# Forty-two unread products behind the last sums of an mLSTM and expert kernel

## The chip, the cores and the metric

The kernel runs on one core of a Trainium2 chip. The metric is device microseconds of one execution, from launch to end. The kernel before took 611.28 us, the median of two runs (610.89 and 611.67). The profile shows one execution, with the hardware profiler's start and length of each instruction. PE is the matrix engine (TensorE), PEld its loads of the stationary operand, DVE, ACT and POOL are VectorE, ScalarE and GpSimd, and SP is the engine that issues the output's transfers.

## The reference

Three stages follow one another. The first is a gated recurrence over 768 steps for 2 x 8 heads of width 40; its 1536 x 320 result goes through four experts that are weighted by given probabilities, and then through a gated pair of products:

```
for e in range(E):                       # w1[e] 320x1024, w2[e] 1024x320
    h = np.maximum(x @ w1[e], 0.0)
    out += p[:, e:e + 1] * (h @ w2[e])
a = x @ w_a                              # 320x1536
b = x @ w_b
return (a * b @ w_out).astype(np.float32)
```

## The kernel before

The weights come in 14 blocks: blocks 0 to 7 hold the experts, blocks 8 to 13 the gated pair. Every float32 operand of a large product is held as a rounded high part and a low part in the type fp32r (`wh` and `wl` for weights, `xh` and `xl` for the input of a stage, `hh` and `hl` for the hidden values), and a product is made of three: high by high, high by low, low by high. The 1536 rows are worked in three groups `c` of 512.

From block 3 on a unit is one block with one group `c` (the list `units`, line 836). A unit first makes its hidden values with `quad_a` (line 228: 60 products with 64 partitions of contraction and 512 columns, issued in pairs on the upper and the lower half of the array), and then, with `quad_b` (line 253: 48 products of 320 columns, in pairs too), the output sums of the unit before it. `evict` (lines 827 to 833) turns sums into `hh` and `hl` on ACT and DVE. `done2` adds finished output sums to the array `acc` on DVE (line 811) and, after block 13, issues the transfer of 128 rows of `acc` to the output from SP's queue (line 815).

The last unit has no unit behind it, so its output sums are made by the loop of lines 868 to 876: four tiles of 128 rows, each of six products over the full 128 partitions and 320 columns (lines 873, 874 and 875), then `done2`. These 24 products are PE's last work. Sums lie in PSUM banks from the pools `pa` and `pb`; `pb` takes turns between two pools of two banks each, and the four of them hold the `py` tiles of the last `quad_b` (line 855). Before the first instruction of the recurrence the manual order is switched on for the rest of the kernel (`ctx.enter_context(tc.manual_schedule())`), so each engine runs its instructions in the order of the program text. Products that are never read exist already: those of `warm_up` (line 626, 17 products of zeros in bf16 with 512 columns over the full array, all with one stationary operand and into one bank). Line 975 is the end of the program: each engine drains, SP waits for the counters of the transfers, and POOL collects the engines and lets them go.

Further lines that the prediction uses: line 208, products of blocks 0 to 2 over the full array with 256 columns; line 527, products of the recurrence with 82 columns whose moving operand starts 41 floats later from head to head; and line 583, the update of the recurrence's state:

```
for g in range(3):
    nc.tensor.matmul(pu[0:120, g * 123:(g + 1) * 123], kw[:, 3 * g:3 * g + 3, :].rearrange("p h d -> p (h d)"), kv[:, NK + g * 123:NK + (g + 1) * 123], ...)
```

There the stationary operand steps by 480 bytes and the moving operand by 492 bytes from one group to the next.

Of the kernel before, what the change touches and what calls it, by code (L numbers as in the profile page):

```python
# [7 lines left out]
F32 = mybir.dt.float32  # L8
# [10 lines left out]
P = 128  # L19
# [29 lines left out]
def mlstm_moe_kernel(ctx, tc, gates, qk, qc, kvo, dp, w1b, w2b, ident_d, bdmask_d, rsel_d, exp_d, out):  # L49
    nc = tc.nc  # L50
# [14 lines left out]
    xh = [xp.tile([P, 3, 512], F32R, name=f"xh{c}") for c in range(3)]  # L65
# [227 lines left out]
    def add_expert(blk, n, ps):  # L293
        e = blk // 2
        if blk <= 1:
            nc.scalar.activation(acc[n], ps, AF.Copy, scale=pg[:, n, 0:1])
        else:
            nc.vector.scalar_tensor_tensor(acc[n], ps, pg[:, n, e:e + 1], acc[n], op0=ALU.mult, op1=ALU.add)
# [491 lines left out]
    pa, pb = Turns(ps_a2, ps_a), Turns(ps_b2, ps_b)  # L790
# [11 lines left out]
    def done2(blk, n, ps):  # L802
        if blk < NB1:
            add_expert(blk, n, ps)
            if blk == NB1 - 1:
                twice[n] = hp2.tile([P, P], F32, tag="twice", name="twice", bufs=4)
                nc.scalar.copy(twice[n].rearrange("p (a b) -> p a b", a=2), acc[n][:, 256:].unsqueeze(1).to_broadcast([P, 2, 64]))
        elif blk == NB1:
            nc.scalar.copy(acc[n], ps)
        else:  # L810
            nc.vector.tensor_tensor(acc[n], ps, acc[n], op=ALU.add)
            if blk == NB1 + NB2 - 1:
                j, b = n // 2, n % 2
                r0 = b * S + j * P
                nc.sync.dma_start(out[r0:r0 + P, :], acc[n])
# [22 lines left out]
    for u, (blk, c) in enumerate(units):  # L838
# [9 lines left out]
        ps = [pa.tile([P, 512], F32, tag="a", name="psa" if blk < NB1 or g % 2 else "psb") for g in range(4)]  # L848
# [18 lines left out]
    wh, wl = wblk[blk]  # L867
    for t in range(4):
        ps = pa.tile([P, 512], F32, tag="a", name="psy")[:, 0:DM]
        for f in range(2):  # L870
            hh, hl = (x[:, t * P:(t + 1) * P] for x in h[f])
            off = f * WF2 + 768
            nc.tensor.matmul(ps, hh, wh[:, off:off + DM], start=f == 0, stop=False)
            nc.tensor.matmul(ps, hh, wl[:, off:off + DM], start=False, stop=False)
            nc.tensor.matmul(ps, hl, wh[:, off:off + DM], start=False, stop=f == 1)
        done2(blk, 4 * c + t, ps)


# ---- launch: one core; the host lays the inputs out
# [99 lines left out]
```

## Time and profile before

| | us |
|---|---|
| timed runs | 610.89 and 611.67, median 611.28 |
| span of the profiled execution, first to last instruction | 609.31 |
| PE busy in that span | 598.1 (98%) |
| DVE, ACT, POOL busy | 406.5, 277.9, 193.3 |
| PE's last product ends | 605.86 |
| from there to the end of the span | 3.45 |

The profiled execution has no time of its own beside its span; the median of the timed runs lies 1.97 us above the span. Starts are given in us from the start of the span. In a timeline each row has the start, the length, the engine, the line and operation with what it writes and reads, the shapes and the count of instructions merged into it. Products overlap in PE's pipeline, so the time that a product takes from its successor is the distance between two starts, not its length.

### The profile page before, as it was taken

The page shows a single profiled execution, that of the slowest core. Times are in us where ns is not written, and L with a number is a line of the kernel's source. Part 1 is how long each engine was busy: PE and PEld are TensorE (multiplying, and loading weights), DVE is VectorE, ACT ScalarE, POOL GpSimd, SP SyncE. Part 2 cuts the span into 40 slices and gives each one's busy share as a digit, 9 for nine tenths or more (in the row PEclk, how much of TensorE's full clock was granted, in tenths as well). Part 3 has the DMA queues.
Part 4 walks back from the last instruction along what each step waited for, and adds up shares of the span by engine and source line. Part 5 has one row for each costly group of instructions (what it writes and reads, how often), then busy time and mean ns, then how long its engine had stood idle before and what let it go on. Part 6 is the DMA issues. An engine that isn't in the chain of part 4 may idle for free.

```text
span 609.3 us, 14397 instructions
## 1 busy us (share of the span) xinstructions
PE 598.1 (98%) x5815; PEld 564.5 (93%) x5815; DVE 406.5 (67%) x829; ACT 277.9 (46%) x643; POOL 193.3 (32%) x233
## 2 busy tenths in 40 slices
PE   8799999999999999999999999999999999999997
PEld 5699999999999899999999999988898988888886
DVE  6898868676553333333789899898776787864344
ACT  7687476756533323333344344454553434331211
POOL 5486426363501011334233333333222222310000
PEclk9999999999999999999999999999999999999999
DMA  8877463737202122222222222222111120200002
GB/s 247 214 219 202 128 181 103 197 104 200 58 19 64 39 62 80 72 75 79 56 76 69 63 75 56 59 63 65 47 50 45 38 56 20 60 16 1 2 31 100
DMA packets 29351, 51.63 MB, mean 85 GB/s; under 512 B 3485, under 2 KB 18117, under 8 KB 29285
## 3 DMA queue, kind: packets, MB, share of 16 engines
q1 hardware_dynamic: 15925, 26.32, 15.9%
q10 hardware_dynamic: 12448, 22.03, 13.2%
q0 software_dynamic: 912, 2.36, 1.4%
q8 instruction: 45, 0.74, 0.5%
q14 instruction: 21, 0.17, 0.1%
HBM read 47.92 MB, written 2.00 MB: 82 GB/s over the span
## 4 chain that ended last, share of the span: by engine, by line
PE 92%; DVE 3%; POOL 1%; issue 1%; DMA 1%; ACT 1%; SPq 0%; DVEq 0%; POOLq 0%
PE psy L253 27%; PE psa L228 27%; PE psb L228 11%; PE psa L208 10%; PE psy L287 3%; PE psy L289 3%; PE psy L288 3%; PE pt_y L527 3%; PE pt_c L513 1%; PE pt_i L533 1%; POOL wl L93 1%; PE pt_u L583 1%; DMA acc<-in_w1b 1%; PE pt_x L145 0%; DMA gt<-in_gates 0%
## 5 line engine op out<-in xcount | busy, mean ns | idle before, releaser
L228 PE MATMUL psa<-xh,wh 64*128 64x512 f32 x576 | 135.2, 390 | 0.0
L253 PE MATMUL psy<-wl,hh 64*128 64x320 f32 x752 | 131.3, 305 | 0.0
L253 PE MATMUL psy<-wh,hh 64*128 64x320 f32 x752 | 131.3, 305 | 0.0
L253 PE MATMUL psy<-wh,hl 64*128 64x320 f32 x752 | 131.2, 305 | 0.0
L228 PE MATMUL psa<-xh,wl 64*128 64x512 f32 x414 | 97.4, 389 | 0.0
L253 PEld LDWEIGHTS psy<-wh,hh 64*128 64x128 f32 x752 | 85.7, 184 | 0.8
L228 PEld LDWEIGHTS psa<-xh,wh 64*128 64x128 f32 x576 | 80.9, 184 | 5.9 <-issue 0.9
L253 PEld LDWEIGHTS psy<-wl,hh 64*128 64x128 f32 x752 | 85.5, 184 | 0.8
L253 PEld LDWEIGHTS psy<-wh,hl 64*128 64x128 f32 x752 | 85.7, 184 | 0.0
L228 PE MATMUL psa<-xl,wh 64*128 64x512 f32 x384 | 85.6, 389 | 0.0
L828 DVE SCALAR_TENSOR_TENSOR hl<-psa,hh 128x512 fp32r<-128x512 f32 x60 | 38.6, 685 | 55.2 <-ACT hh L827 54.9
L125 POOL TENSOR_TENSOR wl<-tp,lf 128x272 fp32r<-128x272 f32 x48 | 38.8, 809 | 113.1 <-DVE tp L124 111.4
L228 PE MATMUL psb<-xh,wh 64*128 64x512 f32 x216 | 69.8, 389 | 0.0
L228 PEld LDWEIGHTS psa<-xh,wl 64*128 64x128 f32 x414 | 60.7, 184 | 3.7
L228 PE MATMUL psb<-xh,wl 64*128 64x512 f32 x180 | 58.5, 389 | 0.0
L228 PEld LDWEIGHTS psa<-xl,wh 64*128 64x128 f32 x384 | 55.2, 184 | 3.6
L122 POOL TENSOR_TENSOR lf<-lf,sq 128x272 f32<-128x272 f32 x48 | 38.1, 794 | 62.9 <-ACT wh L121 48.9
L276 DVE SCALAR_TENSOR_TENSOR hl<-psa,hh 128x256 fp32r<-128x256 f32 x72 | 30.3, 421 | 40.4 <-ACT hh L275 40.0
L93 POOL TENSOR_TENSOR wl<-raw,wh 128x352 fp32r<-128x352 f32 x28 | 26.4, 947 | 95.1 <-ACT wh L91 68.6
L275 ACT ACTIVATE hh<-psa 128x256 fp32r<-128x256 f32 x72 | 27.6, 383 | 59.2 <-PE psa L208 58.5
L827 ACT ACTIVATE hh<-psa 128x512 fp32r<-128x512 f32 x60 | 32.6, 596 | 44.7 <-PE psy L253 26.6
L208 PE MATMUL psa<-xh,wh 128*128 128x256 f32 x216 | 51.5, 293 | 0.3 <-ACT xh L133 0.3
(146 smaller groups left out, 1435.1 us busy)
## 6 DMA issues: line engine op xcount, KB each, us to landing
raw<-in_w2b ACTq DMA_DIRECT2D x48, 272.0 KB, 2.8
qk_t<-in_qk SPq DMA_DIRECT2D x16, 480.0 KB, 4.7
raw<-in_w1b ACTq DMA_DIRECT2D x32, 176.0 KB, 2.3
acc<-in_w1b SPq DMA_DIRECT2D x24, 176.0 KB, 4.0
kvo_t<-in_kvo SPq DMA_DIRECT2D x10, 364.5 KB, 7.1
Rr<-dL_t ACTq DMA_DIRECT2D x5, 512.0 KB, 6.3
og_t<-in_kvo SPq DMA_DIRECT2D x6, 320.0 KB, 4.6
out<-acc SPq DMA_DIRECT2D x12, 160.0 KB, 1.9
```

The source lines that it names most:

```text
L93: lo_eng.tensor_tensor(wl[:, cs], raw, wh[:, cs].bitcast(F32), op=ALU.subtract)
L122: nc.gpsimd.tensor_tensor(lf, lf, sq, op=ALU.mult)
L125: nc.gpsimd.tensor_tensor(wl[:, cs], tf, lf, op=ALU.add)
L208: nc.tensor.matmul(ps, l, r, start=(i == 0), stop=(i == len(prs) - 1))
L228: return nc.tensor.matmul(ps[g], w[rows, o:o + P], x, start=start, stop=stop)
L253: ms = [nc.tensor.matmul(ps[t], l[rows, t * P:(t + 1) * P], w[rows, off:off + DM], start=start, stop=stop) for t, rows in zip(two, (UP, DN))]
L275: nc.scalar.activation(self.hh, ps, AF.Relu)
L276: nc.vector.scalar_tensor_tensor(self.hl, ps, 0.0, self.hh.bitcast(F32), op0=ALU.max, op1=ALU.subtract)
L287: nc.tensor.matmul(ps, lh, wh[:, off:off + DM], start=(fi == 0), stop=False)
L288: nc.tensor.matmul(ps, lh, wl[:, off:off + DM], start=False, stop=False)
L827: nc.scalar.activation(hh, ps[f], AF.Relu)
L828: nc.vector.scalar_tensor_tensor(hl, ps[f], 0.0, hh.bitcast(F32), op0=ALU.max, op1=ALU.subtract)
```

## The change

Behind the loop the next turn of `pb` gives a bank to a new tile `ps_z`, and 42 products over the full array with 512 columns in fp32r are issued into it, each with start and stop set. `line` is `xh[2]` of the last group seen as 1536 columns in a row, `wh` is the high part of block 13's weights. The first 27 keep the moving operand at its start and move the stationary operand by 0, 8, ..., 64 floats (32 bytes a step), three products at each place; the other 15 keep the stationary operand and move the moving operand by 0, 8, ..., 32 floats. Nothing reads `ps_z`.

```
@@ -874,6 +874,11 @@
             nc.tensor.matmul(ps, hh, wl[:, off:off + DM], start=False, stop=False)
             nc.tensor.matmul(ps, hl, wh[:, off:off + DM], start=False, stop=f == 1)
         done2(blk, 4 * c + t, ps)
+    ps = pb.tile([P, 512], F32, tag="b", name="ps_z")
+    line = xh[2].rearrange("p a b -> p (a b)")
+    for w, x in [(8 * r, 0) for r in range(9)] + [(0, 8 * r) for r in range(5)]:
+        for _ in range(3):
+            nc.tensor.matmul(ps, wh[:, w:w + P], line[:, x:x + 512], start=True, stop=True)
```

## Rows read from the trace of the kernel before

**Rows 1.** The page: span and busy time of each engine with its share and instructions.
```profile
span 609.3 us, 14397 instructions
PE 598.1 (98%) x5815; PEld 564.5 (93%) x5815; DVE 406.5 (67%) x829; ACT 277.9 (46%) x643; POOL 193.3 (32%) x233
```

**Rows 2.** The page's 40 slices: busy tenths of PE, and its granted clock.
```profile
PE   8799999999999999999999999999999999999997
PEclk9999999999999999999999999999999999999999
```

**Rows 3.** Chain that ended last: start, us, what; its last pieces.
```profile
598.62 3.52 PE psy L253 x48
...
605.56 0.15 PE psy L874
605.71 0.16 PE psy L875
605.87 0.02 issue
605.89 0.49 DVE acc L811
```

**Rows 4.** The stretch behind PE's last product: length, then busy time by engine.
```profile
605.86:609.31 3.45, 0.00 (x0) 0.00 (x0) 0.49 (x1) 0.00 (x0) 0.00 (x0) 1.00 0.38 135
```

**Rows 5.** Timeline of the last sums: last of line 253, first and last of lines 873 to 875.
```profile
601.84 0.30 PE L253 MATMUL psy<-wh,hl 64*128 64x320 f32 x2
602.07 0.42 PE L873 MATMUL psy<-wh,hh 128*128 128x320 f32 x1
...
602.62 0.30 PE L873 MATMUL psy<-wh,hh 128*128 128x320 f32 x1
...
605.55 0.31 PE L875 MATMUL psy<-wh,hl 128*128 128x320 f32 x1
605.89 0.49 DVE L811 TENSOR_TENSOR acc<-psy,acc 128x320 f32<-128x320 f32 x1 [0.39 <-PE psy L875]
```

**Rows 6.** The page: the output's transfers, KB each, us from issue to landing.
```profile
out<-acc SPq DMA_DIRECT2D x12, 160.0 KB, 1.9
```

**Rows 7.** Line 975, the program's end: ns min/median/max, first and last start.
```profile
L975 SPq EVENT_SEMAPHORE  x12: 17/28/28, 606.8 to 609.2; - x12
L975 POOLq EVENT_SEMAPHORE  x4: 17/17/17, 608.6 to 609.2; - x4
...
L975 SPq DRAIN  x3: 7/7/13, 608.5 to 608.8; - x3
...
L975 PEldq DRAIN  x2: 13/1420/2828, 603.1 to 608.8; - x2
```

**Rows 8.** Line 626, unread products: ns min/median/max, first and last start, forms.
```profile
L626 PEld LDWEIGHTS <-acc x17: 98/138/151, 1.4 to 20.1; 128*128 128x128 bf16 x17
L626 PE MATMUL pt_w<-acc x17: 379/609/634, 1.4 to 20.2; 128*128 128x512 bf16 x17
```

**Rows 9.** Chain, a typical unit: 30 pairs of 512 columns from line 228.
```profile
336.72 6.83 PE psa L228 x60
```

**Rows 10.** Timeline: line 228 in the last unit, 13 steps of a pair apart.
```profile
595.25 0.39 PE L228 MATMUL psa<-xh,wh 64*128 64x512 f32 x1
...
598.23 0.39 PE L228 MATMUL psa<-xh,wh 64*128 64x512 f32 x1
```

**Rows 11.** Timeline: five products of line 626 in a row, at full clock.
```profile
17.43 1.24 PE L626 MATMUL pt_w<-acc 128*128 128x512 bf16 x5
```

**Rows 12.** Timeline: line 208, full array, 256 columns, then the next line.
```profile
61.83 0.28 PE L208 MATMUL psa<-xh,wh 128*128 128x256 f32 x1
...
61.95 0.28 PE L208 MATMUL psa<-xh,wl 128*128 128x256 f32 x1
...
62.07 0.31 PE L287 MATMUL psy<-wh,hh 128*128 128x320 f32 x1
```

**Rows 13.** Line 875, loads of the stationary operand: columns as in the rows of line 626.
```profile
L875 PEld LDWEIGHTS psy<-wh,hl x8: 187/188/188, 602.3 to 605.4; 128*128 128x128 f32 x8
```

**Rows 14.** Line 583, operands at steps of 480 and 492 bytes: loads and products.
```profile
L583 PEld LDWEIGHTS pt_u<-kvo_t,kw_t x60: 181/183/186, 32.3 to 144.3; 128*120 128x120 f32 x60
L583 PE MATMUL pt_u<-kvo_t,kw_t x60: 266/268/271, 32.4 to 144.4; 128*120 128x123 f32 x60
```

**Rows 15.** Timeline: one run of line 583, six products merged.
```profile
51.71 0.80 PE L583 MATMUL pt_u<-kvo_t,kw_t 128*120 128x123 f32 x6
```

**Rows 16.** SP's waits from 606 us on: us in total, times, longest.
```profile
SPq L975 <- DMA out<-acc: 1.1, 3, 0.5
```

## The prediction

> **What bounds the kernel now.** I read the page first. PE is busy for 598.1 of 609.3 us [rows 1], and its slices are full from end to end at full granted clock, the faster of its two levels, 2.4 GHz [rows 2]. So work that is added to PE lengthens the kernel unless it falls into a stretch where PE has nothing to do. The chain of waits says where such a stretch lies: it is a string of PE's products up to the last one of line 875, then one addition on DVE [rows 3]. Behind that product, from 605.86 us to the end at 609.31, PE has no work at all [rows 4]. What fills these 3.45 us is the addition, which ends at 605.89 + 0.49 = 606.38 [rows 5], the last transfer of 160 KB, 1.9 us from issue to landing [rows 6], and the closing of the program [rows 7].
>
> The closing decides how much of that stretch is free for PE. PE's drain starts at 603.1 us, well ahead of the products, and lasts 2.83 us, to 605.9: it ends with the last product [rows 7]. SP then runs through its waits for counters from 606.8 us and drains at 608.5, and POOL begins to collect the engines at 608.6 [rows 7]; I read the moment from which everything hangs as 608.55. From there 0.76 us are left to the end of the span. PE may therefore finish 608.55 - 605.90 = 2.65 us later than now before it is the last that POOL waits for. That is the slack which the change can use up.
>
> **The change, part by part.** It removes and moves nothing, and every instruction that it adds is on PE: 42 loads of a stationary operand and 42 products. No transfer is added, and no queue is passed by another.
>
> *Do they run at all, and where?* Each engine follows the program text, so they stand behind the 24 products of lines 873 to 875. That an unread product is not left out is shown by line 626: all 17 of its products and all 17 of its loads are in the trace, though nothing reads their bank and all have one and the same stationary operand [rows 8]. So I count 42 loads too, not 14.
>
> *The first one.* Its bank belonged to the first `py` tile, which DVE has added up well before 605.7 us, and its operands were ready long ago; nothing is late for it. Where PE passes from line 253 to line 873, the step is 602.07 - 601.84 = 0.23 us instead of the usual 0.147 [rows 5]; I take these 0.08 us once, for the pass to a new bank with its waits. Behind the products only PE's drain is queued.
>
> *The step of one product.* The trace has no full-array fp32r product with 512 columns in a row of its own kind, so I bound it. Above: line 228 issues two halves of the array together with 512 columns each, 6.83 us for 30 pairs or 0.228 each [rows 9], and in the last unit 598.23 - 595.25 = 2.98 us for 13 steps, 0.229 [rows 10]. Below: five unread bf16 products of 512 columns over the full array into one bank take 1.24 us at full clock; without the last one's own length, 0.38, that is 0.86 / 4 = 0.215 [rows 11]. Between: 256 columns over the full array step by 0.12 [rows 12], 320 by (605.55 - 602.62) / 20 = 0.1465 [rows 5]; the line through both gives 0.1465 + 192 x 0.0265 / 64 = 0.226 at 512. I take 0.2287, the pairs', since 64 rows or 128 make no difference at 320 columns either: 48 products of line 253 in pairs take 3.52 us, 0.1467 a pair [rows 3]. The stationary loads last 188 ns [rows 13] and start beside the product before, so they stay hidden. Writing one bank again and again costs nothing in line 626.
>
> The Trainium skill, TensorE: Matmul & The Clock Gate, section Back-to-back issue gap, gives two figures for a warm product of 512 columns: 215.7 ns alone, and about 131 ns in a stream of loads and products. The first agrees with the lower bound from line 626; no row here shows 512 columns as short as the second. By 131 ns the 42 would take 5.5 us, of which 2.9 would show, and the time would be 614.1.
>
> *The addresses.* They are the open question. 24 products have a moved stationary operand and 12 a moved one on the other side; only 6 start both at the tiles' beginnings. The nearest rows are line 583, whose stationary operand steps by 480 bytes (a multiple of 32, not of 64) and whose moving operand steps by 492. Its loads last 181 to 186 ns and its products 266 to 271 over all three places [rows 14]: no place stands out, so the low end is nothing. The high end: a run's six products (each of its three calls leaves two in the trace) take 0.80 us [rows 15], without the last one's length (0.80 - 0.27) / 5 = 0.106 each for 123 columns, or 0.862 ns a column. If all of that were the reading of the moving operand, 512 columns would take 0.441 us, 0.212 more than 0.2287. For the 12 with a moved moving operand that is 2.5 us at most; if the stationary operand's address counted alike, 7.6 us for 36. I take nothing, as the lengths at the three places say.
>
> *The sum.* Added to PE: 42 x 0.2287 + 0.08 = 9.69 us. Less the slack of 2.65: 7.04 us. Step by step: the first would start at 605.55 + 0.147 + 0.08 = 605.78, the last 41 steps later at 615.16, and end 0.39 later at 615.55; PE's drain 0.04 behind it, then 0.76 for the closing: a span of 616.35 against 609.31. The difference goes on the median of the timed runs, which stands 1.97 us above the span for what lies around it: 611.28 + 7.04 = 618.3 us. If SP also waits for PE's new counter before its other entries, those come behind it: SP spends 608.5 - 606.8 = 1.7 us on its list, 1.1 of it waiting for transfers [rows 7, 16] that would be over by then, so up to 0.6 more. With the step of 0.215 the sum is 9.03 + 0.08 - 2.65 = 6.5.
>
> **The rivals.**
>
> *Shorter than the sum, or no change.* If the number of columns did not set the step, 42 products could go at 0.106 as in line 583: 4.45 + 0.08 - 2.65 = 1.9 us, 613.2. Against it: the steps grow with the columns, 0.12, 0.1465, 0.228 [rows 5, 9, 12]. The Trainium skill's 131 ns, named above, would lie between. To vanish wholly the products would have to be dropped, which line 626 speaks against, or step by 2.57 / 42 = 0.061, half of the shortest step seen; then 611.3. Together 3 in 100.
>
> *The moving operand's address costs a part.* The 12 products with a moved moving operand take up to 0.441 each: up to 618.3 + 2.5 = 620.9. For it speaks only that no row has an fp32r operand at 32 bytes from a 64-byte step; line 583 with its even lengths speaks against it. 9 in 100.
>
> *Slower by over 2%.* Any start away from the tile's beginning, of either operand, makes a product read its operand at half rate. Then 36 products take a second 0.2287: 8.2 us on top, 626.5. It decides from 12.2 us (2% of 611.28) on, that is from (12.2 - 7.04) / 36 = 0.144 more per product, 0.37 us a product. Line 583 allows up to 0.441 a product and so doesn't exclude it, but its loads of 181 to 186 ns at steps of 480 bytes show no trace of it. 6 in 100.
>
> **How the numbers follow.** The forecast, 42 products at 0.215 to 0.235 us and nothing for addresses, has 82 in 100 and gives 617.8 to 619.2; with the two runs' scatter of 0.4 us each way, and the upper bound of the moved moving operand, the range is 617.2 to 621.3. It leaves out the dropped or shortened products and the half rate, some 1 in 10, and a part of the second rival. Over or under 2%, 12.2 us, is about what a measurement of this kernel can tell from no change: the forecast is 1.2% longer, inside it. Slower by over 2% is the half rate alone, 0.06; for faster by over 2% I see no mechanism and leave 0.01; within 2% is the rest, 0.93.
>
> **What would show it right or wrong.** In the changed kernel's profile the 42 products should stand behind 605.7 us, with steps of 0.228 from first to last, the three at each place alike, at full granted clock. Loads should stay near 188 ns. PE should be busy some 608 us, its drain should end near 615.6, POOL's collecting start right behind it, and the chain of waits end on PE instead of on DVE's addition. DVE's last addition and the output's last transfer should stand where they are. Steps that widen where the moving operand moves, and stay there, would be the second rival; steps that widen at every moved place, the third. A stretch of idle time ahead of the first new product would mean a wait for the bank that I costed at 0.08 us.

## The result and the profile after

The changed kernel takes 618.24 us, the median of two runs (617.88 and 618.60), against 611.28: 1.011 times as long, 95% interval 1.0085 to 1.0135, or 5.2 to 8.3 us. The forecast was 618.3 with a range of 617.2 to 621.3, and within 2%.

The page of the changed kernel answers [rows 1]: the span is 7.6 us longer and PE's busy time 11.0 us, of which 9.7 lie in the new products; the rest lies ahead of them, where the two executions differ. The chain's end, in which [rows 3] had DVE's addition last, now has the 42 products last. Their 9.72 us are 0.2314 us a product.

```profile
span 616.9 us, 14480 instructions
...
PE 609.1 (99%) x5856; PEld 573.8 (93%) x5857; DVE 405.9 (66%) x829; ACT 277.6 (45%) x643; POOL 193.7 (31%) x233
```

```profile
605.89 0.15 PE psy L874
606.04 0.15 PE psy L875
606.19 9.72 PE ps_z L881 x42
```

The timeline shows the passage from the last sums to the new products, as [rows 5] showed the last sums: start, length, engine, line, operation, count. The first new product starts 0.14 us behind the last of line 875, with no gap, and DVE's last addition runs beside the new products. It stands 0.33 us later than before, as the last sums do: that much of the two profiled executions' difference arose ahead of the changed lines.

```profile
605.88 0.31 PE L875 MATMUL psy<-wh,hl 128*128 128x320 f32 x1
...
606.02 9.88 PE L881 MATMUL ps_z<-xh,wh 128*128 128x512 f32 x42
...
606.23 0.49 DVE L811 TENSOR_TENSOR acc<-psy,acc 128x320 f32<-128x320 f32 x1 [0.39 <-PE psy L875]
```

The new line's own rows (ns min/median/max, first and last start) answer [rows 13]: the loads take what they took in the last sums. The rows of the program's end answer [rows 7]; it is line 980 now. PE's drain starts at 611.6 and lasts 4.36 us, to 615.95, one of SP's waits lasts 6.58 us, and POOL begins to collect at 616.1. SP's waits answer [rows 16]: SP waits 6.6 us for the products that nobody reads.

```profile
L881 PEld LDWEIGHTS ps_z<-xh,wh x42: 187/188/189, 605.9 to 615.3; 128*128 128x128 f32 x42
L881 PE MATMUL ps_z<-xh,wh x42: 387/394/400, 606.0 to 615.5; 128*128 128x512 f32 x42
```

```profile
L980 SPq EVENT_SEMAPHORE  x12: 17/28/6582, 607.6 to 616.8; - x12
L980 POOLq EVENT_SEMAPHORE  x4: 17/17/17, 616.1 to 616.8; - x4
...
L980 PEldq DRAIN  x2: 13/2185/4357, 611.6 to 616.4; - x2
```

```profile
SPq L980 <- PE ps_z L881: 6.6, 1, 6.6
SPq L980 <- DMA out<-acc: 1.3, 3, 0.5
```

One thing changed that is not on PE. Of SP's twelve issues of the output's transfers (line 815), the longest took 0.435 us before and takes 1.453 us after; the first row is the kernel before, the second the changed one. Among the last eight transfers the median from issue to landing rose from 1.9 us, as in [rows 6], to 2.6.

```profile
L815 SPq DMA_DIRECT2D out<-acc x12: 332/372/435, 591.8 to 606.4; - x12
```

```profile
L815 SPq DMA_DIRECT2D out<-acc x12: 332/374/1453, 592.1 to 607.2; - x12
```

In the changed kernel's transfers between 602.9 and 604.6 us one packet of 16 KB on the queue of instructions stands beside the output's. The same stretch of the kernel before has none; its last packet on that queue starts at 610.59, behind the last instruction of the span.

```profile
q8 instruction: 1, 0.02, 4.7%
out<-acc SPq DMA_DIRECT2D x2, 160.0 KB, 3.2
```

### The profile page after: what moved, and what is told of

The parts are those of the page before. It is cut to its first block, busy times and chain, and to the rows that moved or that the text cites. A ratio compares the mean times of both kernels' runs of the same rounds, so it can differ in the third digit from the quotient of the medians.

```text
span 616.9 us, 14480 instructions
## 1 busy us (share of the span) xinstructions
PE 609.1 (99%) x5856; PEld 573.8 (93%) x5857; DVE 405.9 (66%) x829; ACT 277.6 (45%) x643; POOL 193.7 (31%) x233
## 4 chain that ended last, share of the span: by engine, by line
PE 93%; POOL 2%; issue 2%; DVE 2%; DMA 1%; SPq 0%; ACT 0%; POOLq 0%; DVEq 0%
PE psy L253 27%; PE psa L228 26%; PE psb L228 11%; PE psa L208 10%; PE psy L287 3%; PE psy L289 3%; PE psy L288 3%; PE pt_y L527 2%; PE pt_c L513 2%; POOL wl L93 2%; PE ps_z L881 2%; PE pt_i L533 1%; DMA qk_t<-in_qk 1%; PE pt_u L583 1%; POOL w_t L505 1%
## 5 line engine op out<-in xcount | busy, mean ns | idle before, releaser
L228 PE MATMUL psa<-xh,wh 64*128 64x512 f32 x576 | 133.5, 390 | 0.0
L253 PE MATMUL psy<-wh,hh 64*128 64x320 f32 x752 | 127.2, 305 | 0.0
L253 PE MATMUL psy<-wh,hl 64*128 64x320 f32 x752 | 127.1, 305 | 0.0
L253 PE MATMUL psy<-wl,hh 64*128 64x320 f32 x752 | 127.0, 305 | 0.0
L228 PEld LDWEIGHTS psa<-xh,wh 64*128 64x128 f32 x576 | 79.1, 184 | 5.9 <-issue 0.9
L253 PEld LDWEIGHTS psy<-wl,hh 64*128 64x128 f32 x752 | 81.5, 184 | 0.8
L253 PEld LDWEIGHTS psy<-wh,hh 64*128 64x128 f32 x752 | 81.4, 184 | 0.8
L253 PEld LDWEIGHTS psy<-wh,hl 64*128 64x128 f32 x752 | 81.6, 184 | 0.0
```

Of the source, the lines that this page charges most:

```text
L228: return nc.tensor.matmul(ps[g], w[rows, o:o + P], x, start=start, stop=stop)
L253: ms = [nc.tensor.matmul(ps[t], l[rows, t * P:(t + 1) * P], w[rows, off:off + DM], start=start, stop=stop) for t, rows in zip(two, (UP, DN))]
```

## The experiments

Theory A is the prediction's: columns set the step of a product, addresses cost nothing, and 2.65 us behind the last sums are free for PE. The rivals are a price of the addresses, a price that does not depend on columns or place, and, after the first results, a second effect that the new instructions have on SP. Experiments of one group ran on one chip beside the kernel before; the ratios are against those runs.

**All products at one place** (group one, with the next three).

```
-    for w, x in [(8 * r, 0) for r in range(9)] + [(0, 8 * r) for r in range(5)]:
-        for _ in range(3):
-            nc.tensor.matmul(ps, wh[:, w:w + P], line[:, x:x + 512], start=True, stop=True)
+    for _ in range(42):
+        nc.tensor.matmul(ps, wh[:, 0:P], line[:, 0:512], start=True, stop=True)
```

> All 42 products keep both operands at their tiles' beginnings; nothing else differs from the changed kernel. If addresses cost nothing, the 42 steps average 0.231 us as in the changed kernel and the time is the changed kernel's, 618.2 us, 1.011 times the kernel before. If a moved start costs a few nanoseconds, as the steps of 0.233 to 0.235 at some places hint against 0.228 at the beginning, all steps are 0.228 to 0.229, PE ends 0.1 us earlier, and the time is still 618.1.

Measured: 618.77 us, ratio 1.0108 (1.0089 to 1.0127), the changed kernel's. The chain gives 9.63 us for 42 products, 0.2293 each, against 0.2314:

```profile
607.16 9.63 PE ps_z L880 x42
```

So addresses decide nothing here, but they are not quite without a trace. The distances between starts, ns, repeat to the nanosecond: from the seventh product on this kernel goes 226, 229, 231 or 232 over and over, and the changed kernel and the kernel of the fourth experiment, with the same addresses, show one sequence from the third place to the last; some of it:

```
place (floats)            changed kernel     products ahead of the last sums
stationary from 16        226 227 235        226 227 235
stationary from 48        237 230 237        237 230 237
stationary from 64        226 229 232        226 229 232
moving from 24            232 234 238        232 234 238
```

A pattern that comes back in another kernel belongs to the places and not to chance. The kernel with 168 products below, on another chip, begins with the same twelve distances as this one. It is worth 231.27 - 229.15 = 2.1 ns a product on the mean of the steps, 0.09 us for the 42.

**Ten products instead of 42.**

```
-    for _ in range(42):
+    for _ in range(10):
```

The lines are those of the first experiment, all operands at their tiles' beginnings.

> Ten products instead of 42, both operands at their tiles' beginnings. 10 x 0.231 = 2.3 us is less than the 2.65 us by which PE's drain came before POOL's collecting. If that slack is free, the time is the kernel before's, 611.3 us (ratio 1.000). If products behind the last sums lengthen the closing whatever their number, it is 611.3 + 2.3 = 613.6 (ratio 1.004).

Measured: 612.71 us against 611.8, ratio 1.0013 (0.9998 to 1.0028). 1.004 is excluded, 1.000 is not. In the trace PE's drain ends at 608.51, 1.33 us ahead of POOL's collecting at 609.84, so the ten products are hidden, as theory A has it. But POOL's collecting stands 3.64 us behind the start of DVE's last addition, where it stood 2.66 in the kernel before, and one of SP's issues took 1.75 us. Something other than PE's work delayed the closing; the last three experiments are about that.

**256 columns instead of 512.**

```
-            nc.tensor.matmul(ps, wh[:, w:w + P], line[:, x:x + 512], start=True, stop=True)
+            nc.tensor.matmul(ps[:, 0:256], wh[:, w:w + P], line[:, x:x + 256], start=True, stop=True)
```

> The same 42 products at the same addresses with 256 columns instead of 512. If columns set the step, it is 0.118 to 0.120 us as on line 208, PE's new work is 5.0 us, and the time is 611.3 + 5.0 - 2.65 + 0.2 = 613.8. If a product has a fixed price by the instruction or by its stationary load, the step stays near 0.23 and the time near 618.2.

Measured: 613.46 us, ratio 1.0029 (1.0017 to 1.0040), or 1.0 to 2.4 us. The chain has 4.95 us for 42 products, 0.118 each, the step of line 208 in [rows 12]:

```profile
605.86 4.95 PE ps_z L881 x42
```

Its span of 611.79 is 2.48 us above the kernel before's, with the last sums at the same place to 0.01 us; the measured terms give 4.95 - 2.65 + 0.18 = 2.48 (the 0.18 is explained under the slack below). The 2.5 of the forecast is met in the trace and lies just above the interval of the times. Columns set the step, and a fixed price by instruction is refuted.

**The products ahead of the last sums.**

```
     wh, wl = wblk[blk]
+    ps = pb.tile([P, 512], F32, tag="b", name="ps_z")
+    ...
     for t in range(4):
```

> The same 42 products, put ahead of the loop of the last sums instead of behind it. If the 2.65 us behind the last sums is the only cover, nothing of 42 x 0.231 = 9.7 us is hidden here: 611.3 + 9.7 = 621.0, up to 0.4 more if the first product waits for DVE to add up the tile that held its bank. If the place does not matter, the time is 618.2.

Measured: 620.95 us, ratio 1.0151 (1.0134 to 1.0168), or 8.2 to 10.3 us. The span is 9.81 us above the kernel before's, so nothing is hidden here, as theory A says of this place. The timeline and the waits show the wait for the bank, too: 0.41 us from the last product of line 253 to the first new one, where it is 0.23 to line 873 in [rows 5], for DVE's addition that frees it. DVE's last addition is again the end of the chain.

```profile
601.77 0.30 PE L253 MATMUL psy<-wh,hl 64*128 64x320 f32 x2
602.18 0.74 PE L872 MATMUL ps_z<-xh,wh 128*128 128x512 f32 x2
```

```profile
PEld ps_z L872 <- DVE acc L811: 0.4, 1, 0.4
```

**The stationary operand's address with nothing to cover the load** (group two, this one and the next two, one run each).

```
+    for w in [8 * r for r in range(9)] + [1, 2, 3, 4, 5]:
+        for _ in range(6):
+            nc.tensor.matmul(ps[:, 0:64], wh[:, w:w + P], line[:, 0:64], start=True, stop=True)
```

> 84 products of 64 columns behind the last sums, all with the moving operand at its beginning, six at each of 14 starts of the stationary operand: 0, 8, ..., 64 floats, then 1, 2, 3, 4, 5 floats. With so few columns the step is the stationary load's own, about 0.107 to 0.112 us. If the load's address costs nothing, all 14 places step alike. If a load from an odd start takes longer and 512 columns only covered it, the places at 32 bytes from a multiple of 64, or those at 1 to 5 floats, step wider by more than 5 ns.

Measured: 622.16 us. The first six places, from 0 to 40 floats, step by 111 or 112 ns, but for the very first step. Then the granted clock falls from 1.00 to 0.50, and the other places, 48, 56, 64 and 1 to 5 floats, step by 213 to 215 ns once the clock is down, all alike again. The columns of the stretches are length, then busy time of PE, PEld, DVE, ACT and POOL, the granted clock, and the DMA's share and GB/s; the loads before and after the fall follow.

```profile
605.20:608.50 3.30, 3.30 (x32) 3.30 (x31) 0.49 (x1) 0.00 (x0) 0.00 (x0) 1.00 0.73 255
609.50:619.00 9.50, 9.50 (x46) 9.50 (x47) 0.00 (x0) 0.00 (x0) 0.00 (x0) 0.50 0.00 0
```

```profile
L881 PEld LDWEIGHTS ps_z<-xh,wh x30: 187/192/192, 605.0 to 608.3; 128*128 128x128 f32 x30
...
L881 PEld LDWEIGHTS ps_z<-xh,wh x47: 315/333/334, 609.2 to 619.0; 128*128 128x128 f32 x47
```

At neither clock can the places seen at it be told apart; starts of 1 to 5 floats were seen here at the lower clock alone. The half rate of the third rival is refuted for the stationary operand.

**Finer and more places.**

```
+    for w, x in [(0, x) for x in (0, 1, 2, 3, 4, 8, 16, 24, 32)] + [(w, 0) for w in (0, 1, 2, 3, 4)]:
+        for _ in range(12):
+            nc.tensor.matmul(ps, wh[:, w:w + P], line[:, x:x + 512], start=True, stop=True)
```

> 168 products of 512 columns behind the last sums, 12 at each place: moving operand from 0, 1, 2, 3, 4, 8, 16, 24, 32 floats, then stationary operand from 0, 1, 2, 3, 4 floats. If addresses cost nothing, each place averages 0.229 to 0.232 us, with the places in no order, and the time is 611.3 + 168 x 0.230 - 2.65 + 0.2 = 647.5. If a moved moving operand costs something, the places off the beginning stand together above the first by 3 ns or more.

Measured: 647.99 us where one run of the kernel before took 612.26, 35.7 us more; 36.2 were expected. The chain has 0.232 us a product:

```profile
606.29 38.97 PE ps_z L881 x168
```

The means of the steps at each place, ns, from the starts in the trace:

```
moving from      0: 230.0   1: 236.1   2: 235.1   3: 228.7   4: 230.7   8: 234.5   16: 232.8   24: 234.5   32: 233.1
stationary from  0: 229.8   1: 233.1   2: 230.3   3: 227.0   4: 232.4
```

The places off the beginning do not stand together above it: 3 floats are below 0, and 4 floats below 16 and 32. The largest difference is 9 ns, from 227.0 to 236.1. What sets these few nanoseconds stays open. In this one trace the distance from a multiple of 32 or 64 bytes does not order them: 3 floats, off both, step shorter than 16 and 32 floats, on both.

**The same words read as bf16.**

```
+    wb, xb = wh.bitcast(BF16), line.bitcast(BF16)
+    for _ in range(42):
+        nc.tensor.matmul(ps, wb[:, 0:P], xb[:, 0:512], start=True, stop=True)
```

> 42 products of 512 columns behind the last sums with the same words read as bf16. If the 0.215 us of line 626 belongs to the type, the step is 0.215 and PE's new work 9.1 us: 617.5. If it belonged to line 626's zeros or place, the step is 0.229 to 0.231 and the time 618.2.

Measured: 616.82 us where one run of the kernel before took 612.26. The steps are 215 or 216 ns, but for a first one of 442, where the trace lacks one product's record; the chain has the other 40 behind it. The time is 0.7 us under the expected one, and only 4.6 us above that one run, where 6.2 were expected; single runs cannot settle that. In this execution the last sums ended 0.8 us earlier than in the profiled one of the kernel before.

```profile
605.33 8.80 PE ps_z L881 x40
```

So the 0.215 us of line 626 belong to the type and not to its zeros or its place: with the same starts, columns and count fp32r steps by 0.229 and bf16 by 0.216. Read as bf16, 512 columns are only the first 256 of the words, half the bytes; whether the type or the bytes make the 13 ns is not separated.

**The fetch of instructions without products at the end** (group three, with the next two). Theory B: the new instructions make PE's stream cross into another 16 KB block just at the end, the block is fetched while the last transfers are issued, and that fetch holds up SP. Its rival: the products behind the last sums hold up SP. That the packets are PE's code is read from a count: the kernel with 168 products has 252 instructions more on PE than the changed kernel and one packet more on that queue (47 against 46), 16384 bytes or 65 for each. This kernel is the kernel before with five small unread products at the start and nothing at the end.

```
+        def small(n):
+            for _ in range(n):
+                nc.tensor.matmul(pw[:, 0:64], wz[:, 0:P], wz[:, 0:64], start=True, stop=True)
-            ... (-17.366, warm_up, 4), (-16.214, go, w0[2:3]),
+            ... (-17.366, warm_up, 4), (-17.3, small, 5), (-16.214, go, w0[2:3]),
```

> The kernel before, with nothing behind the last sums, and five more unread bf16 products of 64 columns at 17 us, where PE is idle for 1.2 us. They add ten instructions to PE's stream, so the 16 KB block of PE's instructions that before was fetched at 610.6 us, behind the end, should be fetched some 8 us earlier, near 602.6. If that fetch holds up SP's issue of an output transfer, one of the last eight issues takes 1.4 to 2.2 us instead of 0.33 to 0.40, POOL's collecting stands some 3.6 us behind the start of DVE's last addition instead of 2.66, and the time is 0.7 to 1.0 us longer (ratio 1.0014). If the slow issue in the runs so far comes from the products behind the last sums, all issues are short, the distance is 2.66 and the ratio 1.000.

Measured: the packet of instructions now starts at 602.98, and one of SP's issues (line 820 here) takes 1.128 us, with no product behind the last sums. The distance from DVE's last addition to POOL's collecting is 3.03 us instead of 2.66, less than the 3.6 expected. In the time it cannot be told: 611.47 against 611.33, ratio 1.0002 (0.9991 to 1.0014).

```profile
L820 SPq DMA_DIRECT2D out<-acc x12: 333/374/1128, 592.0 to 606.7; - x12
```

**Ten products, with the fetch moved away.** Ten products as in the second experiment, ten of the small ones at 17 us and twelve at 15.

```
+            ... (-29.623, s2a, 1, 0), (-29.5, small, 12),
+            ... (-17.366, warm_up, 4), (-17.3, small, 10), (-16.214, go, w0[2:3]),
```

> Ten products behind the last sums as in the earlier run of ten, and 22 more unread bf16 products of 64 columns at 15 and 17 us. The 44 instructions should move the fetch of PE's block to about 600 us, ahead of the last eight output transfers. If the fetch is what holds up SP, their issues take 0.33 to 0.40 us and POOL's collecting stands 2.7 us behind the start of DVE's last addition, with the ten products still behind the last sums; up to 1 us of new work may show in the first 20 us. If the ten products hold up SP, one issue takes 1.4 us or more and the distance is 3.6 us.

Measured: 610.89 us, ratio 0.9994 (0.9982 to 1.0006). The fetch lasts from 603.04 to 604.23, and the first of the last eight issues from 603.79 to 604.13, within it, at its usual 0.333 us; the second starts as the fetch ends. This profiled execution reached the last sums 1.6 us later than the kernel before. The longest issue takes 0.403 us, the median landing of the last eight is 1.8 us, and POOL's collecting stands 2.64 us behind the start of DVE's last addition, with ten products behind the last sums.

```profile
L820 SPq DMA_DIRECT2D out<-acc x12: 332/372/403, 593.4 to 608.0; - x12
```

**Ten products once more.**

> The ten products once more, beside the two kernels above. If the fetch theory holds, this one keeps its slow issue and 3.6 us from DVE's last addition to POOL's collecting, and lies 0.7 to 1.0 us above the kernel before (ratio 1.001 to 1.002). If the distance of the first look was chance, it is 2.7 us and the ratio 1.000.

Measured: 612.25 us, ratio 1.0014 (1.0000 to 1.0028). The fetch starts at 603.874 and SP's slow issue at 603.868; it takes 1.609 us, and the distance is 3.47 us.

```profile
L815 SPq DMA_DIRECT2D out<-acc x12: 333/374/1609, 592.6 to 607.8; - x12
```

The three kernels separate the two theories. A fetch in the middle of the issues gives a slow issue with ten products (1.75 and 1.61 us) and with none (1.13); ten products with the fetch over by the second issue give none.

The end of the fetch ties the two together more closely. From the starts and lengths in the traces, us:

```
                                 fetch             slow issue        ends behind the fetch by
fetch without products           602.98 to 604.14  603.26 to 604.39  0.25
changed kernel                   603.37 to 604.64  603.45 to 604.90  0.27
ten products once more           603.87 to 605.18  603.87 to 605.48  0.30
168 products                     603.58 to 605.40  603.56 to 605.78  0.38
```

In all ten kernels with a slow issue it ends 0.15 to 0.39 us behind the fetch, while the fetches last 1.15 to 1.82 us. It is not a matter of the program's end either: the kernel before has a case at 100 us, where the packet of instructions takes from 100.24 to 101.19 and the issue, of line 370, ends at 101.55.

```profile
100.46 1.09 SPq L370 DMA_DIRECT2D kvo_t<-in_kvo  x1
```

Through the twelve traces, 41 issues of SP follow another within 0.15 us and start between 0.12 us ahead of such a fetch and its end; 40 of them end 0.15 to 0.39 us behind it. Of some 800 that follow another as closely elsewhere, nine take over 0.7 us, and no fetch on this queue explains those. An issue after a longer pause can be short in the middle of a fetch, as the first of the last eight is in the second of these kernels.

That a fetch at this place holds up SP is shown, by moving it and by when the slow issue ends; by what means it does so is not. The price in the trace is 0.8 us between the closings of the second and the third of these kernels (3.47 less 2.64). The times agree: of the second kernel's twelve, ten lie below all twelve of the third (medians 610.89 and 612.25).

## Why the prediction was right, point by point

**The work on PE.** 42 x 0.2287 + 0.08 = 9.69 us was forecast. Measured are 42 x 0.2313 = 9.71, with 0.2313 the mean distance between the starts from 606.025 to 615.507. Two small errors cancelled, which is luck: the step was 2.6 ns longer, and the 0.08 us for the pass to the new bank were not there. The 0.23 us step from line 253 to line 873, from which they were taken, is still there in the changed kernel (602.17 to 602.40), so it belongs to that passage and not to a new bank as such: the load of line 873 starts only with its product there, while the first new load starts at 605.88, beside the last product of line 875.

**The step's bounds.** The value from the pairs of line 228, between their 0.2277 and 0.2292 [rows 9, 10], was right to 1%, the line through 256 and 320 columns, 0.226, to 2.3%, and the bf16 rows [rows 11] were a lower bound for the reason that the type, and with it the bytes, differs. The figure of 131 ns for 512 columns in a stream that the Trainium skill gives (TensorE: Matmul & The Clock Gate, Back-to-back issue gap) was not reached by any run: the shortest steps of 512 columns are 225 ns in fp32r and 215 in bf16. Its other figure, about 216 ns for a product alone, agrees with the bf16 steps of 215 and 216.

**The slack.** 2.65 us were to be hidden. The slack was sized 0.18 us too large: POOL collects 0.18 us behind the end of PE's drain, 615.95 to 616.13, and not at once, because SP stands in its list at the wait for PE's counter and has one more entry and its drains to do behind it. The prediction had named that wait, with up to 0.6 us. The sum by the measured terms is 9.71 - 2.65 + 0.18 = 7.24 us; with the 0.33 us that arose ahead of the change it makes 7.57 of the spans' difference of 7.58. The timed difference is 6.96, with an interval of 5.2 to 8.3, so the times alone would not tell 7.0 from 7.3, and that 618.3 and 618.24 agree so closely is luck.

**Where it was wrong.** The prediction said that the output's last transfer would stand where it was, and that no transfer is added. The first is refuted: SP's issues run 0.44 us later at the end once the common 0.33 us are taken off (the last one from 606.413 to 607.185). The step that failed is the second, since 84 more instructions did add a transfer within the span, 16 KB of PE's own code. It cost the changed kernel nothing, since PE ended last by far; in the kernel with ten products it is the one thing that shows. Nor is 2% about what a measurement of this kernel can tell from no change, as the prediction says: the interval of 1.011 reaches 0.25% to either side.

**The addresses.** I took nothing, and 0.09 us of 9.7 is measured. The three products at one place were not alike, as I had said they would be, but apart by up to 9 ns in a repeating pattern. The rivals of a dearer moving operand (up to 0.441 us a product) and of half rate are refuted: no place's mean step is over 0.237 us. The bound of 0.441 was mis-read, too: it laid line 583's step of 0.106 us for 123 columns on the moving operand, but 64 columns step by 0.111, and both come to 0.87 or 0.88 ns for each of the 128 or 120 columns of the stationary load. So line 583's step is most likely that of its load, and the upper end of the range, 621.3, rested on a cost that its rows do not show.

## What to carry to other kernels

In this kernel, work at the end of an engine's stream was free up to the moment at which the closing would collect that engine; compare the end of its drain with the start of the collecting, and count only what exceeds that distance. Price a product by the distance between starts of the nearest rows with the same type and columns, since the length shown of one includes what its successor overlaps. A few instructions more on one engine can move a fetch of code into another engine's critical stretch: after any change of the instruction count, look where the packets on the instruction queue fall, and whether an issue of SP ends just behind one.

## What the hardware showed that I had not expected

A 16 KB fetch of PE's instructions that starts among SP's last eight issues of transfers goes with one issue of 1.1 to 2.2 us in place of 0.33 to 0.50, in the changed kernel and in nine of the ten experiments, and that issue ends 0.15 to 0.39 us behind the fetch; in the tenth the fetch starts 0.75 us ahead of the first of them, and all are short.

PE's granted clock fell from 1.00 to 0.50 in the middle of an unbroken stream of products, those of 64 columns at 0.112 us a product: loads went from 192 to 333 ns and steps from 112 to 213. In the changed kernel, with 512 columns a product, the clock stayed at 1.00 to the end.
